# Two pairs of chunks at once through an FFN, with one PSUM bank left to the attention beside it

## The chip, the cores and the metric

The kernel runs on one core of a Trainium2 chip. The metric is the device time of one execution in microseconds (us), the median of several runs.

## The reference, cut to what matters

```python
# q, k, v: (4, 8, 768, 64) float32; w_in: 512 x 2048, w_out: 2048 x 512, handed over as float64
def _attn_ref(q, k, v):
    gamma = 1.0 - 2.0 ** (-5.0 - np.arange(H))
    for t in range(S):
        state = gamma[None, :, None, None] * state + np.einsum('bhd,bhe->bhde', k[:, :, t], v[:, :, t])
        y[:, :, t] = scale * np.einsum('bhd,bhde->bhe', q[:, :, t], state)
    ...
def _moe_ref(x, w_in, w_out):
    h = x @ w_in
    g = np.maximum(h, 0.0) + np.log1p(np.exp(-np.abs(h)))
    return (g @ w_out).astype(np.float32)
    ...
# x is y with its heads side by side: 3072 tokens x 512
```

A linear attention with a decay for each head is followed by a two-layer FFN with softplus between its layers.

## The kernel before

**Attention.** The 3072 tokens are 24 chunks of 128 (six for each of the four sequences). A chunk is worked in two halves of four heads; such a half is a *unit*, and there are 48, numbered in order. Within a unit, q times k gives scores, which are masked and multiplied by v; the state that came from earlier chunks is multiplied by q and added (`yp`); k times v is added up in PSUM (`stp`) as the next state. Units below `WHOLE` (12) do this in plain fp32 with transposes on TensorE. Later units split each operand into a high and a low part (fp32r) and sum the products; their q and k come as 32x32 blocks by small DMAs, 16 for a unit, and are transposed on VectorE. A unit's result is written into the ring `xring` as a high part `xh` and a low part `xl`.

**FFN.** `hidden(s)` multiplies a chunk of `w_in` (128 of the 2048 columns, `f`) with the tokens of one block in the ring, three products (high-high, high-low, low-high) for each of the four slices of 512, into a PSUM tile `hp`. `softplus(s)` makes `gh` and `gl` of it on VectorE, ScalarE and GpSimd. `second(s)`, run two steps later (`LAG`), multiplies these with `w_out` into accumulators of 128 tokens x 512. The blocks of tokens are 256, 256, six times 384, and 256 (`BLOCKS`). A step has two `f` for a block of 256 and one for 384, so 120 steps in all. Block 0 is interrupted: it goes through the first ten `f`, then block 1 runs through all 16 while the last weights arrive, then block 0 takes the rest and adds a stored partial sum. The weights come as float64 and are converted in pieces of one `f` (`convert_weights`), which takes all the engines but TensorE.

**PSUM.** Eight banks: two for `hp`, three accumulators `acc0` to `acc2`, two for the attention (`ps_a`, tag `a`, used in turn by transposes, scores and `yp`), one for the states.

**Order.** Attention runs in *ticks*: `PARTS` says at which tick of a unit each part of it comes (loads 24 ticks ahead or, from `THIRD` on, 40; operands at 0, scores at 8, new state at 12, outputs at 19 or 20), and a new unit begins every 16 ticks. The main loop walks over the FFN's steps and lets the ticks pass between them. For the first 32 steps (`ordered`), up to the end of block 2, a `plan` says how far the ticks are to get by each step, and a scheduler orders the instructions of every engine by a model of their times. From step 32 on the order of TensorE's instructions is fixed as written (`manual_schedule`), and `paced` deals out the ticks over the pieces of the steps, where a piece is one turn of `hidden` or of `second`, three matmuls. The other engines' orders come from the scheduler throughout.

Of the kernel before, what the change touches and what calls it, by code (L numbers as in the profile page):

```python
# [19 lines left out]
BLOCKS = (256, 256) + 6 * (384,) + (256,)  # L20
RING = 768
SPREAD = 9
# [5 lines left out]
TURN = 5  # L28
# [6 lines left out]
def decay_attention_then_softplus_ffn(ctx: ExitStack, tc: tile.TileContext, q, k, v, w_in, w_out, qtab, vtab, gtab, out):  # L35
# [7 lines left out]
    assert sum(BLOCKS) == B * S  # L43
    FIRST = np.cumsum((0,) + BLOCKS)
# [8 lines left out]
    ps_a = ctx.enter_context(tc.tile_pool(name="ps_a", bufs=2, space=bass.MemoryType.PSUM))  # L53
# [52 lines left out]

    xring = [attn.tile([P, ND, RING], F32R, name=nm) for nm in ("xh", "xl")]
    places, spans = {}, {}
    for i, size in enumerate(BLOCKS):
        at = (0, 256, 384, 0)[i] if i < 4 else 384 * (i % 2 == 0)  # L110
        order = {2: (1, 2, 0), 3: (2, 0, 1)}.get(i, range(size // C))
        spans[i] = slice(at, at + size), order
        for m, pos in enumerate(order):
            places[int(FIRST[i]) // C + m] = at + pos * C
# [17 lines left out]

    def block_tile(nm, n):
        home = {"pool": ffn, "tag": "part"} if n >= THIRD and (n - THIRD) % 3 == 0 else {"pool": attn, "tag": nm}
        if n < THIRD - 2:
            return home["pool"].tile([P, NJ, C // 32, 32], F32, name=f"{nm[0]}b", tag=home["tag"], bufs=2)
        at = nm, (n - THIRD) % 3
        if at not in rings:
            rings[at] = home["pool"].tile([P, NJ, C // 32, 32], F32, name=f"{nm[0]}b", tag=home["tag"], bufs=2)
        return rings[at]  # L140
# [27 lines left out]
    def load_ahead(n):  # L168
        if n >= THIRD:
            load_qk(n)  # L170
# [35 lines left out]

    def operands(n):
        b, c, hf = units[n]
        *rest, vn = loads.pop(n)
        if n < WHOLE:  # L210

            tp = ps_o.tile([P, 2, NJ, C], F32, name="tp", tag=f"acc{n % 2}") if n < 4 else ps_a.tile([P, 2, NJ, C], F32, name="tp", tag="a")
# [27 lines left out]
    def scores(n):  # L240
        kq = live[n][0]
        a = attn.tile([P, HH, C], F32, name="a")
        if n < WHOLE:
            sc = ps_a.tile([P, HH, C], F32, name="sc", tag="a")
            for h in range(HH):
                nc.tensor.matmul(sc[:, h, :], lhsT=kz[:, h % 2, h // 2, :], rhs=kq[:, h // 2, :], start=True, stop=True)
            nc.scalar.copy(a, sc)
        else:
            for j in range(NJ):
                sc = ps_a.tile([P, 2, 2, C], F32, name="sc", tag="a")  # L250
                for par in range(2):
                    nc.tensor.matmul(sc[:, par], lhsT=kq[:, 0, par, j, :], rhs=kq[:, 1:, par, j, :], start=True, stop=True)  # L252
                nc.vector.tensor_reduce(a[:, 2 * j:2 * j + 2, :], sc.rearrange("p h t c -> p h c t"), axis=mybir.AxisListType.X, op=ALU.add)  # L253
        nc.gpsimd.affine_select(a, a, pattern=[[0, HH], [1, C]], compare_op=ALU.is_ge, fill=0.0, base=0, channel_multiplier=-1)  # L254
        live[n].append(a)
        if n >= WHOLE:
            ah, al = (attn.tile([P, HH, C], F32R, name=nm) for nm in ("ah", "al"))
            nc.scalar.copy(ah, a)  # L258
            nc.gpsimd.tensor_tensor(al, a, ah.bitcast(F32), op=ALU.subtract)  # L259
            live[n][-1:] = [ah, al]  # L260
# [37 lines left out]
    def outputs(n):  # L298
        b, c, hf = units[n]
        kq, *rest, st = live.pop(n)  # L300
        off, g = places[n // 2], hf * NJ
        xh, xl = (x[:, g:g + NJ, off:off + C] for x in xring)
        if n < WHOLE:
            kn, vn, a = rest
            yp = ps_a.tile([P, NJ, C], F32, name="yp", tag="a")
# [10 lines left out]
        yp = ps_a.tile([D, 2, NJ, C], F32, name="yp", tag="a")  # L316
# [23 lines left out]
        ys = vn.rearrange("p h d -> p (h d)").rearrange("p (j c) -> p j c", j=NJ)  # L340
# [10 lines left out]

    def outputs_soon(n):
        if n >= WHOLE:
            stack_and_outputs(n)

    def outputs_late(n):
        if n < WHOLE:
            stack_and_outputs(n)

    PARTS = {-24: load_unit, -40: load_ahead, -8: decay, 0: operands, 8: scores, 12: new_state, 19: outputs_soon, 20: outputs_late}  # L360
# [11 lines left out]

    acc, part, hps, sps, gs = {}, {}, {}, {}, {}

    def hidden(s):
        i, fs = steps[s]
        xh, xl = (x[:, :, spans[i][0]] for x in xring)
        hp = hps[s] = ps_h.tile([P, len(fs), BLOCKS[i]], F32, name="hp", tag="hp")
        for k, d in ((k, d) for k in range(len(fs)) for d in range(ND)):
            wt = win[fs[k]].rearrange("p t (c f) -> p t c f", c=ND)  # L380
            nc.tensor.matmul(hp[:, k], lhsT=wt[:, 0, d, :], rhs=xh[:, d, :], start=d == 0, stop=False)  # L381
            nc.tensor.matmul(hp[:, k], lhsT=wt[:, 0, d, :], rhs=xl[:, d, :], start=False, stop=False)  # L382
            nc.tensor.matmul(hp[:, k], lhsT=wt[:, 1, d, :], rhs=xh[:, d, :], start=False, stop=d == ND - 1)  # L383
            yield
# [15 lines left out]

    def second(s):
        i, fs = steps[s]
        NT = BLOCKS[i] // P
        gh, gl = gs.pop(s)
        begins = s == 0 or steps[s - 1][0] != i
        ends = s + 1 == len(steps) or steps[s + 1][0] != i
        if begins:
            acc[i] = [ps_o.tile([P, DM], F32, name=f"acc{t}", tag=f"acc{t}") for t in range(NT)]
        for k, t in ((k, t) for k in range(len(fs)) for t in range(NT)):
            wt, ts = wout[fs[k]], slice(t * P, (t + 1) * P)  # L410
            nc.tensor.matmul(acc[i][t], lhsT=gh[:, k, ts], rhs=wt[:, 0], start=begins and k == 0, stop=False)  # L411
            nc.tensor.matmul(acc[i][t], lhsT=gh[:, k, ts], rhs=wt[:, 1], start=False, stop=False)  # L412
            nc.tensor.matmul(acc[i][t], lhsT=gl[:, k, ts], rhs=wt[:, 0], start=False, stop=ends and k == len(fs) - 1)  # L413
            if ends and (k, t) == (len(fs) - 1, NT - 1):
                write_out(i, fs)
            yield

    def write_out(i, fs):
        NT = BLOCKS[i] // P
        for t in range(NT):  # L420
            if fs[-1] < NF - 1:
                part[i, t] = ffn.tile([P, DM], F32, name="part")
                (nc.scalar.copy if t % 2 else nc.vector.tensor_copy)(part[i, t], acc[i][t])
                continue
            o = ffn.tile([P, DM], F32, name="o", tag="o")
            if (i, t) in part:
                nc.vector.tensor_tensor(o, acc[i][t], part.pop((i, t)), op=ALU.add)
            else:
                (nc.scalar.copy if t % 2 else nc.vector.tensor_copy)(o, acc[i][t])
            row = int(FIRST[i]) + list(spans[i][1]).index(t) * P  # L430
            nc.sync.dma_start(out[row:row + P, :], o)

    turns = [(0, 0, 2 * TURN), (1, 0, NF), (0, 2 * TURN, NF)]
    turns += [(i, 0, NF) for i in range(2, len(BLOCKS))]
    steps = []
    for i, a, b in turns:
        m = WIDE // BLOCKS[i]
        steps += [(i, tuple(range(f, f + m))) for f in range(a, b, m)]  # L440

    def ticks_for(i):

        return min(PERIOD * 2 * int(FIRST[i + 1] // C) + max(PARTS) - PERIOD + TICK + TICK * AHEAD, last_tick + TICK)

# [64 lines left out]
    starts = [s for s, (i, fs) in enumerate(steps) if fs[0] == 0]  # L510
    ordered = starts[3]
    plan = [0] * ordered
    for i in 1, 2, 3:
        a, b = starts[i - 1], starts[i]
        a, n = {1: (a + 1, b - a - 2), 2: (b - SPREAD, SPREAD), 3: (a + 1, b - a - 2)}[i]
        have, more = ticks_for(i - 1), ticks_for(i) - ticks_for(i - 1)
        for s in range(a, b):
            plan[s] = have + more // TICK * min(s - a + 1, n) // n * TICK

    def pieces_of(s):
        return len(steps[s][1]) * ND + len(steps[s - LAG][1]) * (BLOCKS[steps[s - LAG][0]] // P)

    paced = {}
    for a, b in zip(starts[3:], starts[4:]):
        i = steps[b][0]
        slots = [(s, t) for s in range(a + 1, b - 1) for t in range(pieces_of(s))]
        have, more = ticks_for(i - 1), ticks_for(i) - ticks_for(i - 1)
# [35 lines left out]
    for s, (i, fs) in enumerate(steps[:ordered]):  # L565
# [39 lines left out]
```

## Time and profile before

| | |
|---|---|
| median of 3 runs | 680.1 us (678.86 to 681.18) |
| the profiled execution | 680.08 us, span 678.4 us |
| granted TensorE clock, mean | 0.997 |
| TensorE busy (PE) | 659.6 us, 97% |
| VectorE, ScalarE, GpSimd busy | 413.0, 369.3, 313.9 us |
| DMA | 46.76 MB, most of it in the first 140 us |

The span is the profiled time from the first to the last instruction; the execution's own time is 1.7 us more. PE counts matmuls and PEld the loading of their stationary operands, which runs beside them. Matmuls are pipelined: a recorded one lasts longer than the distance to the next one, so the price of one in a stream is the distance from start to start. "<-" behind an idle time names what ended it. The ends of the slices on the page are 17 us apart.

### The profile page before, as it was taken

How to read it: one execution, taken by the hardware profiler on the slowest of the kernel's cores; microseconds unless marked ns; L12 is line 12 of the kernel's file. 1: busy time of each engine (PE TensorE's matmuls, PEld its weight loads, DVE VectorE, ACT ScalarE, POOL GpSimd, SP SyncE). 2: the span in 40 equal slices, each digit the busy share in tenths (PEclk: the TensorE clock that was granted, in tenths of full speed). 3: DMA queues.
4: the chain of work that ended last, by engine and by line, in shares of the span. 5: the costliest groups of instructions: out<-in, count | busy, mean ns of one | idle time of the engine just before them, and what ended most of it. 6: DMA issues, size and time to landing. Idle time of an engine off the chain costs nothing.

```text
span 678.4 us, 12865 instructions
## 1 busy us (share of the span) xinstructions
PE 659.6 (97%) x4146; PEld 600.6 (89%) x4146; DVE 413.0 (61%) x807; ACT 369.3 (54%) x844; POOL 313.9 (46%) x354
## 2 busy tenths in 40 slices
PE   7999899999999999999999999999999999999997
PEld 6888789997988898999999999999999899999996
DVE  5778698567566766674757655775666645432321
ACT  5878775545645555663656545654555635423221
POOL 5787666534534543534453525454435443232221
PEclk9999999999999999999999999999999999999999
DMA  9898652123221232221322222131322101000100
GB/s 241 222 287 238 186 141 65 26 70 76 53 39 37 46 88 38 42 45 36 78 47 38 49 66 45 31 57 34 79 38 52 23 8 56 1 1 1 46 1 32
DMA packets 153827, 46.76 MB, mean 69 GB/s; under 512 B 140448, under 2 KB 148640, under 8 KB 153760
## 3 DMA queue, kind: packets, MB, share of 16 engines
q1 hardware_dynamic: 153312, 45.93, 28.4%
q8 instruction: 33, 0.54, 0.3%
q14 instruction: 34, 0.28, 0.1%
q10 hardware_dynamic: 448, 0.01, 0.0%
HBM read 39.60 MB, written 6.29 MB: 68 GB/s over the span
## 4 chain that ended last, share of the span: by engine, by line
PE 62%; DMA 10%; DVE 8%; ACT 7%; SPq 5%; issue 4%; POOL 2%; ACTq 0%; DVEq 0%; POOLq 0%
PE hp L381 9%; PE acc L412 9%; PE acc L413 9%; PE acc L411 9%; PE hp L382 9%; PE hp L383 9%; SPq L150 4%; PE yp L322 4%; DMA win<-in_moe_w_in_dram 3%; DMA qb<-in_q_dram 2%; DMA kb<-in_k_dram 2%; PE sc L252 2%; DMA vn<-in_v_dram 1%; PE stp L274 1%; DMA qn<-in_q_dram 1%
## 5 line engine op out<-in xcount | busy, mean ns | idle before, releaser
L398 POOL TENSOR_TENSOR gl<-sp,gh 128x384 fp32r<-128x384 f32 (+1 forms) x120 | 129.9, 1083 | 213.0 <-ACT gh L396 182.7
L381 PE MATMUL hp<-xh,winhl 128*128 128x384 f32 (+1 forms) x576 | 186.9, 325 | 2.1 <-DVE sp L394 1.6
L383 PE MATMUL hp<-xh,winhl 128*128 128x384 f32 (+1 forms) x576 | 184.1, 320 | 0.0
L382 PE MATMUL hp<-xl,winhl 128*128 128x384 f32 (+1 forms) x576 | 183.4, 318 | 0.0
L411 PE MATMUL acc<-wouthl,gh 128*128 128x512 f32 x384 | 151.6, 395 | 0.0
L412 PE MATMUL acc<-wouthl,gh 128*128 128x512 f32 x384 | 151.2, 394 | 0.0
L413 PE MATMUL acc<-wouthl,gl 128*128 128x512 f32 x384 | 150.8, 395 | 0.2 <-POOL gl L398 0.2
L390 ACT ACTIVATE sp<-sp 128x384 f32<-128x384 f32 (+1 forms) x120 | 65.5, 546 | 135.7 <-DVE sp L389 133.4
L381 PEld LDWEIGHTS hp<-xh,winhl 128*128 128x128 f32 x576 | 108.8, 189 | 6.0 <-DVE sp L394 1.4
L382 PEld LDWEIGHTS hp<-xl,winhl 128*128 128x128 f32 x576 | 109.0, 189 | 3.4
L389 DVE TENSOR_SCALAR sp<-hp 128x384 uint32<-128x384 uint32 (+1 forms) x120 | 68.9, 575 | 67.8 <-PE hp L383 66.5
L383 PEld LDWEIGHTS hp<-xh,winhl 128*128 128x128 f32 x576 | 108.7, 189 | 0.2
L396 ACT CAST gh<-sp 128x384 fp32r<-128x384 f32 (+1 forms) x120 | 64.2, 535 | 75.1 <-DVE sp L394 54.2
L394 DVE SCALAR_TENSOR_TENSOR sp<-hp,sp 128x384 f32<-128x384 f32 (+1 forms) x120 | 69.2, 577 | 38.3 <-ACT sp L390 37.7
L413 PEld LDWEIGHTS acc<-wouthl,gl 128*128 128x128 f32 x384 | 71.8, 188 | 15.6 <-POOL gl L398 0.4
L412 PEld LDWEIGHTS acc<-wouthl,gh 128*128 128x128 f32 x384 | 72.2, 188 | 10.9
L411 PEld LDWEIGHTS acc<-wouthl,gh 128*128 128x128 f32 x384 | 72.2, 188 | 10.8
L254 POOL TENSOR_SCALAR_AFFINE_SELECT a<-a 128x512 f32<-128x512 f32 x48 | 35.7, 744 | 55.8 <-DVE a L253 49.6
L259 POOL TENSOR_TENSOR al<-a,ah 128x512 fp32r<-128x512 f32 x36 | 47.3, 1313 | 7.5 <-ACT ah L258 7.5
L224 DVE STREAM_TRANSPOSE kb<-kb 128x256 f32<-128x256 f32 x36 | 16.0, 445 | 56.6 <-DMA kb<-in_k_dram 46.0
L253 DVE TENSOR_REDUCE a<-sc 128x256 f32<-128x512 f32 x72 | 47.1, 681 | 5.2 <-PE sc L252 4.6
L258 ACT CAST ah<-a 128x512 fp32r<-128x512 f32 x36 | 22.3, 619 | 42.9 <-POOL a L254 42.9
(80 smaller groups left out, 912.1 us busy)
## 6 DMA issues: line engine op xcount, KB each, us to landing
win<-in_moe_w_in_dram SPq DMA_DIRECT2D x16, 512.0 KB, 4.6
wout<-in_moe_w_out_dram SPq DMA_DIRECT2D x16, 512.0 KB, 4.4
vn<-in_v_dram SPq DMA_DIRECT2D x48, 128.0 KB, 2.3
out_dram<-o SPq DMA_DIRECT2D x24, 256.0 KB, 2.1
kb<-in_k_dram SPq DMA_DIRECT2D x288, 16.0 KB, 1.7
qb<-in_q_dram SPq DMA_DIRECT2D x288, 16.0 KB, 1.7
vn<-in_k_dram SPq DMA_DIRECT2D x30, 128.0 KB, 2.3
qn<-in_q_dram SPq DMA_DIRECT2D x12, 128.0 KB, 4.2
```

The costliest lines, as they stand in the source:

```text
L259: nc.gpsimd.tensor_tensor(al, a, ah.bitcast(F32), op=ALU.subtract)
L381: nc.tensor.matmul(hp[:, k], lhsT=wt[:, 0, d, :], rhs=xh[:, d, :], start=d == 0, stop=False)
L382: nc.tensor.matmul(hp[:, k], lhsT=wt[:, 0, d, :], rhs=xl[:, d, :], start=False, stop=False)
L383: nc.tensor.matmul(hp[:, k], lhsT=wt[:, 1, d, :], rhs=xh[:, d, :], start=False, stop=d == ND - 1)
L389: nc.vector.tensor_scalar(sp.bitcast(U32), hps[s].bitcast(U32), 0x80000000, None, op0=ALU.bitwise_or)
L390: nc.scalar.activation(sp, sp, AF.Softplus)
L394: nc.vector.scalar_tensor_tensor(g, hps.pop(s), 0.0, g, op0=ALU.max, op1=ALU.add)
L396: nc.scalar.copy(gh, g)
L398: nc.gpsimd.tensor_tensor(gl, sps.pop(s), gh.bitcast(F32), op=ALU.subtract)
L411: nc.tensor.matmul(acc[i][t], lhsT=gh[:, k, ts], rhs=wt[:, 0], start=begins and k == 0, stop=False)
L412: nc.tensor.matmul(acc[i][t], lhsT=gh[:, k, ts], rhs=wt[:, 1], start=False, stop=False)
L413: nc.tensor.matmul(acc[i][t], lhsT=gl[:, k, ts], rhs=wt[:, 0], start=False, stop=ends and k == len(fs) - 1)
```

## The change

The tokens go in *pairs* of chunks, 256 tokens, of which there are 12. A turn of the FFN has two pairs in flight, so that a hidden matmul has 512 columns, and the two are half of the weights apart: in a turn over the first eight `f` (or the last eight) one pair ends and the next one begins. Pair 0 alone takes the first eight, pair 1 alone all 16, then pairs 0 and 2 the last eight, 2 and 3 the first eight, 3 and 4 the last, and so on, up to pair 11, which ends alone. There are 96 steps. Each pair in flight has two accumulators, so four banks hold accumulators, and one is left to the attention from unit 12 on. For the units before that the fourth accumulator's bank is the attention's second. The scores come in two parts, at ticks 7 and 10, and the outputs all come at tick 20. TensorE's order is fixed from step 12 on (the third turn). The results before splitting (`ys`) get a buffer of their own from unit 19 on, in place of `vn`; each tile of the result is written out as soon as its last matmul is in.

```diff
-BLOCKS = (256, 256) + 6 * (384,) + (256,)
-RING = 768
+TWO = 2 * C
+PLACES = 3
-TURN = 5
+TURN = 4
...
-    ps_a = ctx.enter_context(tc.tile_pool(name="ps_a", bufs=2, space=bass.MemoryType.PSUM))
+    ps_a = ctx.enter_context(tc.tile_pool(name="ps_a", bufs=1, space=bass.MemoryType.PSUM))
...
+    xring = [attn.tile([P, ND, PLACES * TWO], F32R, name=nm) for nm in ("xh", "xl")]
+    def place_of(p):
+        return p if p < PLACES else (1, 0, 2)[p % PLACES]
...
     def load_ahead(n):
-        if n >= THIRD:
+        if n > THIRD:
             load_qk(n)
...
+    def attention_bank(n, shape, name):
+        taken.append(n)
+        if n < WHOLE and len(taken) % 2:
+            return ps_o.tile(shape, F32, name=name, tag="acc3")
+        return ps_a.tile(shape, F32, name=name, tag="a")
...
+    def scores_of_pair(n, j):
+        kq = live[n][0]
+        if j == 0:
+            summed[n] = attn.tile([P, HH, C], F32, name="a")
+        sc = attention_bank(n, [P, 2, 2, C], "sc")
+        for par in range(2):
+            nc.tensor.matmul(sc[:, par], lhsT=kq[:, 0, par, j, :], rhs=kq[:, 1:, par, j, :], start=True, stop=True)
+        nc.vector.tensor_reduce(summed[n][:, 2 * j:2 * j + 2, :], sc.rearrange("p h t c -> p h c t"), axis=mybir.AxisListType.X, op=ALU.add)
...
-        yp = ps_a.tile([D, 2, NJ, C], F32, name="yp", tag="a")
+        yp = attention_bank(n, [D, 2, NJ, C], "yp")
...
-        ys = vn.rearrange("p h d -> p (h d)").rearrange("p (j c) -> p j c", j=NJ)
+        if n < THIRD:
+            ys = vn.rearrange("p h d -> p (h d)").rearrange("p (j c) -> p j c", j=NJ)
+        else:
+            ys = rings[("kn", "qn")[n % 2]].rearrange("p j i d -> p j (i d)")
...
-    PARTS = {-24: load_unit, -40: load_ahead, -8: decay, 0: operands, 8: scores, 12: new_state, 19: outputs_soon, 20: outputs_late}
+    PARTS = {-24: load_unit, -40: load_ahead, -8: decay, 0: operands, 7: scores_first, 8: scores_whole, 10: scores_second, 12: new_state, 20: stack_and_outputs}
...
+    turns = [((0,), 0, 2 * TURN), ((1,), 0, NF), ((0, 2), 2 * TURN, NF)]
+    turns += [((p, p + 1), *((0, 2 * TURN), (2 * TURN, NF))[p % 2]) for p in range(2, PAIRS - 1)]
+    turns += [((PAIRS - 1,), 2 * TURN, NF)]
+    for pairs, a, b in turns:
+        starts.append(len(steps))
+        m = WIDE // (len(pairs) * TWO)
+        steps += [(pairs, tuple(range(f, f + m))) for f in range(a, b, m)]
...
     def hidden(s):
-        i, fs = steps[s]
-        xh, xl = (x[:, :, spans[i][0]] for x in xring)
+        pairs, fs = steps[s]
+        at = sorted(place_of(p) for p in pairs)
+        at = slice(at[0], at[-1] + 1, max(1, at[-1] - at[0]))
+        xh, xl = (x.rearrange("p d (r t) -> p d r t", t=TWO)[:, :, at] for x in xring)
...
     def second(s):
+        for p in pairs:
+            if begins(s, p):
+                odd = p % 2 or p == 0
+                acc[p] = [ps_o.tile([P, DM], F32, name=f"acc{t}", tag=f"acc{t}") for t in ((0, 1) if odd else (2, 3))]
...
+            if last:
+                write_out(p, t, s < TURN)
...
-    ordered = starts[3]
+    ordered = starts[2]
...
-    for a, b in zip(starts[3:], starts[4:]):
-        i = steps[b][0]
-        slots = [(s, t) for s in range(a + 1, b - 1) for t in range(pieces_of(s))]
-        have, more = ticks_for(i - 1), ticks_for(i) - ticks_for(i - 1)
+    for p in range(3, PAIRS):
+        slots = [(s, t) for s in range(starts[p - 1], starts[p]) for t in range(pieces_of(s))]
+        have, more = ticks_for(p - 1), ticks_for(p) - ticks_for(p - 1)
         for t, slot in enumerate(slots):
             paced[slot] = have + more * (t + 1) // len(slots)
```

More of the change, by code (lines that the diff above doesn't have):

```diff
@@ L133, in block_tile @@
     def block_tile(nm, n):
-        home = {"pool": ffn, "tag": "part"} if n >= THIRD and (n - THIRD) % 3 == 0 else {"pool": attn, "tag": nm}
         if n < THIRD - 2:
-            return home["pool"].tile([P, NJ, C // 32, 32], F32, name=f"{nm[0]}b", tag=home["tag"], bufs=2)
+            return attn.tile([P, NJ, C // 32, 32], F32, name=f"{nm[0]}b", tag=nm, bufs=2)
         at = nm, (n - THIRD) % 3
         if at not in rings:
-            rings[at] = home["pool"].tile([P, NJ, C // 32, 32], F32, name=f"{nm[0]}b", tag=home["tag"], bufs=2)
+            if n == THIRD:
+                both = ffn.tile([P, 2, NJ, C // 32, 32], F32, name=f"{nm[0]}bys", tag="part")
+                rings[at], rings[nm] = both[:, 0], both[:, 1]
+            else:
+                rings[at] = attn.tile([P, NJ, C // 32, 32], F32, name=f"{nm[0]}b", tag=nm, bufs=2)
         return rings[at]
@@ L210, in operands @@
         if n < WHOLE:
-            tp = ps_o.tile([P, 2, NJ, C], F32, name="tp", tag=f"acc{n % 2}") if n < 4 else ps_a.tile([P, 2, NJ, C], F32, name="tp", tag="a")
+            tp = ps_o.tile([P, 2, NJ, C], F32, name="tp", tag=f"acc{n % 2}") if n < 4 else attention_bank(n, [P, 2, NJ, C], "tp")
             for t, x in enumerate(rest):
@@ L238, in operands, with mask, scores_whole @@
         live[n] = [kq, vhl, tokens_of(n)[1], vn]
-    def scores(n):
+    def mask(a):
+        nc.gpsimd.affine_select(a, a, pattern=[[0, HH], [1, C]], compare_op=ALU.is_ge, fill=0.0, base=0, channel_multiplier=-1)
+    def scores_whole(n):
+        if n >= WHOLE:
+            return
         kq = live[n][0]
         a = attn.tile([P, HH, C], F32, name="a")
-        if n < WHOLE:
[L244 to L260, printed above, removed]
@@ new lines, in scores_whole @@
+        sc = attention_bank(n, [P, HH, C], "sc")
+        for h in range(HH):
+            nc.tensor.matmul(sc[:, h, :], lhsT=kz[:, h % 2, h // 2, :], rhs=kq[:, h // 2, :], start=True, stop=True)
+        nc.scalar.copy(a, sc)
+        mask(a)
+        live[n].append(a)
+    summed = {}
+    def scores_of_pair(n, j):
[6 more added lines that the diff above has]
+        nc.vector.tensor_reduce(summed[n][:, 2 * j:2 * j + 2, :], sc.rearrange("p h t c -> p h c t"), axis=mybir.AxisListType.X, op=ALU.add)
@@ L262, in decay_attention_then_softplus_ffn, with scores_first, scores_second @@
+    def scores_first(n):
+        if n >= WHOLE:
+            scores_of_pair(n, 0)
+    def scores_second(n):
+        if n < WHOLE:
+            return
+        scores_of_pair(n, 1)
+        a = summed.pop(n)
+        mask(a)
+        ah, al = (attn.tile([P, HH, C], F32R, name=nm) for nm in ("ah", "al"))
+        nc.scalar.copy(ah, a)
+        nc.gpsimd.tensor_tensor(al, a, ah.bitcast(F32), op=ALU.subtract)
+        live[n] += [ah, al]
     began = {}
@@ L401, in second @@
     def second(s):
-        i, fs = steps[s]
-        NT = BLOCKS[i] // P
+        pairs, fs = steps[s]
         gh, gl = gs.pop(s)
[L405 to L415, printed above, removed]
-            yield
@@ L418, in write_out @@
[L418 to L431, printed above, removed]
@@ L435, in decay_attention_then_softplus_ffn @@
[L435 to L444, printed above, removed]
+        places = sorted(place_of(p) for p in pairs)
+        for p in pairs:
+            if begins(s, p):
+                odd = p % 2 or p == 0
+                acc[p] = [ps_o.tile([P, DM], F32, name=f"acc{t}", tag=f"acc{t}") for t in ((0, 1) if odd else (2, 3))]
@@ new lines, in second @@
+        for k, p, t in ((k, p, t) for k in range(len(fs)) for p in pairs for t in range(2)):
+            at = places.index(place_of(p)) * TWO + t * P
+            first, last = begins(s, p) and k == 0, ends(s, p) and k == len(fs) - 1
+            wt, ts, to = wout[fs[k]], slice(at, at + P), acc[p][t]
+            nc.tensor.matmul(to, lhsT=gh[:, k, ts], rhs=wt[:, 0], start=first, stop=False)
+            nc.tensor.matmul(to, lhsT=gh[:, k, ts], rhs=wt[:, 1], start=False, stop=False)
+            nc.tensor.matmul(to, lhsT=gl[:, k, ts], rhs=wt[:, 0], start=False, stop=last)
+            if last:
+                write_out(p, t, s < TURN)
+            yield
@@ new lines, in write_out @@
+    def write_out(p, t, partial):
+        to = acc[p][t]
+        if partial:
+            part[t] = ffn.tile([P, DM], F32, name="part")
+            (nc.scalar.copy if t % 2 else nc.vector.tensor_copy)(part[t], to)
+            return
+        o = ffn.tile([P, DM], F32, name="o", tag="o")
+        if p == 0:
+            nc.vector.tensor_tensor(o, to, part.pop(t), op=ALU.add)
+        else:
+            (nc.scalar.copy if t % 2 else nc.vector.tensor_copy)(o, to)
+        row = p * TWO + t * P
+        nc.sync.dma_start(out[row:row + P, :], o)
@@ L563, in paced_stages @@
                 slot += 1
-    for s, (i, fs) in enumerate(steps[:ordered]):
+    for s, (pairs, fs) in enumerate(steps[:ordered]):
         if s == TURN:
```

52 lines of the change are left out of this document (22 added, 30 removed).

## The prediction

> **What bounds the kernel now.** I read the page first (span, busy time, the slices), then busy time by stretch, then single matmuls in the timeline, then the waits around the one PSUM tile that the change takes a bank from.
>
> ```profile
> span 678.4 us, 12865 instructions
> ...
> PE 659.6 (97%) x4146; PEld 600.6 (89%) x4146; DVE 413.0 (61%) x807; ACT 369.3 (54%) x844; POOL 313.9 (46%) x354
> ...
> PE   7999899999999999999999999999999999999997
> ```
>
> TensorE is the bound: 97% of the span, and nines nearly throughout. The other engines are at 46 to 61%. So only two things count: how long the stream of matmuls is, and how long TensorE stands still in it. The time by stretch (columns: PE, PEld, DVE, ACT, POOL busy, each with its instructions; granted clock; DMA share; GB/s):
>
> ```profile
> 0.00:20.00 20.00, 15.91 (x82) 13.74 (x83) 10.71 (x31) 11.30 (x23) 11.43 (x25) 0.91 0.95 254
> 20.00:100.00 80.00, 74.86 (x540) 68.78 (x540) 63.90 (x113) 63.89 (x135) 57.97 (x70) 1.00 0.76 209
> 100.00:120.00 20.00, 20.00 (x133) 18.34 (x132) 17.25 (x30) 11.73 (x21) 14.46 (x13) 1.00 0.34 79
> 120.00:300.00 180.00, 175.24 (x1108) 158.85 (x1107) 118.55 (x234) 100.73 (x245) 82.68 (x91) 1.00 0.25 51
> 300.00:565.00 265.00, 264.03 (x1635) 241.67 (x1635) 165.38 (x338) 147.59 (x357) 116.51 (x129) 1.00 0.22 47
> 565.00:678.40 113.40, 109.59 (x658) 99.27 (x656) 37.26 (x64) 34.02 (x67) 30.88 (x29) 1.00 0.04 14
> ```
>
> Idle TensorE is the stretch less its PE column: 4.1 us in the first 20, 5.1 us to 100, none to 120, 4.8 us from 120 to 300, 1.0 us to 565, and 3.8 us at the end, which is the last write-out. The granted clock is 1.00 after the first 20 us, so no part of this is a slow clock. The kernel could be freed of some 10 us of idle at most; the rest has to come out of the stream.
>
> **The stream.** The start of a matmul to the start of the next one is its price (the recorded durations overlap):
>
> ```profile
> 401.09 0.40 PE L411 MATMUL acc<-wouthl,gh 128*128 128x512 f32 x1
> ...
> 401.79 0.34 PE L381 MATMUL hp<-xh,winhl 128*128 128x384 f32 x1
> ...
> 402.86 0.33 PE L381 MATMUL hp<-xh,winhl 128*128 128x384 f32 x1
> 647.95 0.28 PE L381 MATMUL hp<-xh,winhl 128*128 128x256 f32 x1
> ...
> 649.03 0.28 PE L381 MATMUL hp<-xh,winhl 128*128 128x256 f32 x1
> L381 PE MATMUL hp<-xh,winhl 128*128 128x384 f32 x384 | 131.9, 344 | 0.0
> L381 PE MATMUL hp<-xh,winhl 128*128 128x256 f32 x192 | 55.0, 287 | 2.1 <-DVE sp L394 1.6 <-ACT xh L313 0.5
> ```
>
> Three of 512 columns lie between 401.09 and 401.79, so 0.233 us each; six of 384 between 401.79 and 402.86, 0.178 each; nine of 256 between 647.95 and 649.03, 0.120 each. The price is about 0.44 ns for a column and 8 to 9 ns for being a matmul. The number of columns does not change: every token meets every weight as before. The number of matmuls does. Before there are 3 x 384 = 1152 of 384 columns and 3 x 192 = 576 of 256 (the two rows, and as many in lines 382 and 383), 1152 x 0.178 + 576 x 0.120 = 274.2 us. After, single pairs run for 8, 16 and 8 of the weight columns' chunks, 32 x 12 = 384 matmuls of 256, and ten two-pair turns of 8 chunks, 10 x 8 x 12 = 960 of 512: 960 x 0.233 + 384 x 0.120 = 269.8 us. That is **4.4 us less**. The second product keeps its 1152 matmuls of 512. That two pairs can lie apart in the ring (places 0 and 2) makes the moving operand a two-level one; the score matmul at line 252 reads such an operand already, and I put it at nothing.
>
> The Trainium skill, page "TensorE: Matmul & The Clock Gate", section "Wait — 56ns, not 53.3ns?", gives a warm matmul N/2.4 GHz and a fixed 2.5 ns or so. By that estimate the 384 matmuls saved would be worth about 1 us. The rows above show more than three times that fixed part here, and the sum goes by them.
>
> **Softplus and gl.** 96 steps instead of 120, each over 512 elements; less work for DVE, ACT and POOL, none of it on the path, as idle TensorE of 1.0 us in the 265 us from 300 on shows. Nothing. The same holds for write-out: an accumulator comes up again only one turn later with hidden matmuls between.
>
> **Fixed order from step 12 instead of step 32.** Step 12 will start near 118 us, where before the scheduler's order went on to about 232 us. The stretch from 120 to 300 lost 4.8 us, and a stall also costs the pipeline's refill, 0.395 - 0.233 = 0.16 us (the 512-column matmul's record against its price; 395 is the mean of one at line 411). With some eight stalls that is 6 us. From 300 to 565 the order was fixed and lost 1 us. If the new order is as smooth, **6 us go**.
>
> **One bank for attention.** This is the cost. In the fixed part every unit now takes its scores of pair j=0, of pair j=1 and its yp from one bank in turn; before there were two. So the next unit's first scores wait until ACT has copied yp out (line 342), and the second scores until DVE has reduced the first (line 253). In a turn of two pairs there are 8 steps of 8 pieces (4 hidden, 4 second) and 64 ticks, one tick behind each piece. yp stands at tick 20, the next unit's first scores at 16 + 7 = 23: three pieces later. Both lie in the second half of the same step, so three pieces are nine matmuls of 512, 9 x 0.233 = 2.10 us. How long does the copy take? Before, a unit at the same place, behind the first second piece of its step:
>
> ```profile
> 320.19 0.40 PE L322 MATMUL yp<-al,vhl 128*64 128x128 f32 x4
> 320.43 0.45 PE L411 MATMUL acc<-wouthl,gh 128*128 128x512 f32 x1
> ...
> 319.39 0.52 ACT L390 ACTIVATE sp<-sp 128x384 f32<-128x384 f32 x1 [2.47 <-DVE sp L389]
> 319.97 0.41 ACT L231 CAST kq<-qb 64x256 fp32r<-64x256 f32 x1
> 320.40 0.40 ACT L232 CAST kq<-qb 64x256 fp32r<-64x256 f32 x1
> 320.82 0.40 ACT L231 CAST kq<-qb 64x256 fp32r<-64x256 f32 x1
> 321.25 0.53 ACT L294 CAST st<-stp 64x128 fp32r<-64x128 f32 x2
> 321.81 0.41 ACT L232 CAST kq<-qb 64x256 fp32r<-64x256 f32 x1
> 322.24 0.74 ACT L342 COPY vn<-yp 64x256 f32<-64x256 f32 x2
> ...
> 323.46 0.63 PE L252 MATMUL sc<-kq 128*128 128x256 f32 x4
> 323.89 0.69 DVE L253 TENSOR_REDUCE a<-sc 128x256 f32<-128x512 f32 x1
> ```
>
> The last yp matmul leaves at 320.43, but ACT first casts the q blocks of the unit after the next (lines 231 and 232, free as soon as yp's state products have read them) and the new state (line 294), 2.2 us in all, and the two copies end at 322.98. That is 2.55 us behind yp. Nothing waited, since the scores at 323.46 went into the other bank. In the new place the scores would come at 320.43 + 2.10 = 322.53 and stand until about 323.05, some 0.5 us. The softplus ahead on ACT is longer with 512 elements, so I take 0.55 us. This queue forms where the unit has state products, stacks a new state, and has the q blocks loaded far ahead: units 18 to 45 are 28, less the 4 of a sequence's first chunk and the 4 of its last, 20 units. 20 x 0.55 = **11 us more**. The waits of before, in which only the second scores came behind yp, five ticks later, were short:
>
> ```profile
> who waited for it (us, times):
>   PEld sc L252: 1.6, 3
>   PE sc L252: 0.9, 1
> ```
>
> That is the whole wait of the scores for line 342, in three places. Lower bound of the new term: these 0.9 us. Upper bound: every one of 36 units at 0.55 and the odd write-out cast (0.58) in half of them, 30 us. I take 11, the counted case.
>
> The Trainium skill, page "PSUM — Partial Sum Buffer", section "Summary: rules for kernel authors", says that to read PSUM while a matmul runs one gives the matmul another bank. The rows above agree: copies and the next scores stand apart by bank before. By this rule the change is a cost in each unit.
>
> The reduce between the two scores: scores start 323.46, reduce ends 324.58, 1.12 us. The new distance is two scores (0.24) and 2.10, 2.34 us. It is covered unless DVE is 1.2 us behind; DVE is busy 62% from 300 to 565, so sometimes. 0 to 8 us, I take 2. From the second scores to yp there remain ten ticks, some 8 us, for
>
> ```profile
> L254 POOL TENSOR_SCALAR_AFFINE_SELECT a<-a 128x512 f32<-128x512 f32 x48 | 35.7, 744 | 55.8 <-DVE a L253 49.6
> L259 POOL TENSOR_TENSOR al<-a,ah 128x512 fp32r<-128x512 f32 x36 | 47.3, 1313 | 7.5 <-ACT ah L258 7.5
> L258 ACT CAST ah<-a 128x512 fp32r<-128x512 f32 x36 | 22.3, 619 | 42.9 <-POOL a L254 42.9
> ```
>
> and the reduce, 0.74 + 1.31 + 0.62 + 0.68 = 3.4 us: covered.
>
> **Units 12 to 17 in fixed order.** Their blocks are still loaded 24 ticks ahead, and late loads now stop TensorE instead of being stepped round:
>
> ```profile
> DVE kb L224 <- DMA kb<-in_k_dram: 46.0, 27, 3.6
> POOL vn L205 <- DMA vn<-in_v_dram: 25.4, 21, 5.9
> ```
>
> Waits of up to 3.6 and 5.9 us, today beside other work. On SP the 16 block loads of a unit stand one behind the other as before. Between nothing and 10 us for six units; I take 3, since most such waits have cover of a few ticks. The separate buffer for ys frees vn sooner, so the load of v no longer waits for line 344: worth nothing after 300 us. The moves by a tick (first scores 8 to 7, second to 10, outputs 19 to 20) pass no DMA of their own: these parts issue only matmuls and the ACT, DVE and POOL work costed above, and the loads that SP issues stay at their ticks, four behind the outputs instead of five.
>
> **The early part.** Turn 0 has 4 steps instead of 5, so the last weights are needed one step sooner, and a step of 256 columns is 24 x 0.120 + 12 x 0.233 = 5.7 us:
>
> ```profile
> L99 ACT CAST winhl<-w x16: 601/620/625, 13.3 to 116.2; 128x512 fp32r<-128x512 f32 x16
> L99 ACT CAST wouthl<-w x16: 601/620/631, 16.5 to 120.3; 128x512 fp32r<-128x512 f32 x16
> ```
>
> The last weights are cast at 116.2 and 120.3 us, just before use, with DVE at 17.25 of 20 us there. If the conversions can't come sooner TensorE stands up to 5.7 us; if they can, nothing (a gain is excluded, all of this work stays). I take 2.
>
> **The sum.** The profiled execution took 680.08 us (span 678.4 and 1.7 around it), which is the median of the runs, 680.1. 680.1 - 4.4 - 6 + 11 + 2 + 3 + 2 = **687.7 us**, slower by 1.1%.
>
> **The rivals.** (1) *The copy is in time.* If ACT's order comes out with the copies ahead of the casts, as they need only 0.74 us, the bank is free 1.3 us before the scores. The point is 2.10 us from yp's end to the copies' end. Then the 11 us vanish and most of the other waits with them: 680.1 - 4.4 - 6 + 1 = about 671 us, faster. For it: the waits of 0.9 us before. Against it: the casts stood ahead by readiness, which this change does not touch. Chance 0.30. (2) *Late operands stop TensorE.* Fixed order starts while loads and conversions still compete; the 3 + 2 + 2 us become 10 + 6 + 8: about 705 us. For it: the waits of up to 5.9 us. Against it: 1 us idle in 265 us of fixed order. Chance 0.10. (3) *Gain and wait cancel.* The wait is met in half of the units only: 680.1 - 10.4 + 6 + 5 = 681 us. Chance 0.13.
>
> **How the numbers follow.** The forecast has chance 0.47, own range 682 to 700. A change of under 0.3% (678 to 682 us) can't be told from none here. Slower 0.47 + 0.10 = 0.57; same 0.13; faster 0.30. The range that leaves out a tenth at each end reaches into both neighbours, 669 to 702 us.
>
> **What would show it.** 1344 hidden matmuls with 512-column ones 0.23 us apart; TensorE waits at line 252 for ACT's line 342, some 20 of about half a us, in the fixed part; little idle between 120 and 300 us beyond these; the last weights' casts near 114 to 118 us with TensorE waiting for them. I am wrong if line 342 runs ahead of lines 231 and 232, or ends within 2.1 us of yp: then the time falls to about 671.

## The result, and the profile after

The changed kernel took 702.7 us (700.0 to 704.9), the kernel before 679.8: 1.033 times as long, 95% interval 1.029 to 1.038. It was forecast slower, but by 1.1%; the time lies 15.0 us above the forecast of 687.7 and 0.7 us above the range of 669 to 702. The changed kernel's page, the lines that answer to those shown of before:

```profile
span 700.0 us, 11837 instructions
...
PE 662.1 (95%) x3762; PEld 556.8 (80%) x3762; DVE 417.4 (60%) x756; ACT 361.1 (52%) x799; POOL 310.1 (44%) x330
...
PE   7899998789899989999999989999999999999997
```

There are 384 fewer matmuls (3762 for 4146), but TensorE's busy time did not fall, because matmuls behind a wait or at a slow clock are busy longer (both are shown below). TensorE is idle 37.9 us where it was 18.8. Of the 19.1 us that came on top, most have one owner. What the changed kernel's copies of yp (line 374, line 342 before) held up:

```profile
who waited for it (us, times):
  PEld sc L273: 28.3, 26
  PE sc L273: 17.0, 25
```

The second line counts idle TensorE: 17.0 us in 25 waits, where before it was 0.9 us in one. By the prediction's estimate each wait costs 0.16 us more for the pipeline to fill again, so some 21 us in all. One of them in detail, ScalarE first, then TensorE:

```profile
354.51 0.63 ACT L432 ACTIVATE sp<-sp 128x512 f32<-128x512 f32 x1 [3.11 <-DVE sp L431]
355.05 0.39 ACT L241 CAST kq<-qb 64x256 fp32r<-64x256 f32 x1
355.46 0.41 ACT L242 CAST kq<-qb 64x256 fp32r<-64x256 f32 x1
355.89 0.40 ACT L241 CAST kq<-qb 64x256 fp32r<-64x256 f32 x1
356.32 0.53 ACT L323 CAST st<-stp 64x128 fp32r<-64x128 f32 x2
356.88 0.41 ACT L242 CAST kq<-qb 64x256 fp32r<-64x256 f32 x1
357.30 0.74 ACT L374 COPY kbys<-yp 64x256 f32<-64x256 f32 x2
```
```profile
355.40 0.45 PE L456 MATMUL acc<-wouthl,gh 128*128 128x512 f32 x1
...
357.31 0.40 PE L458 MATMUL acc<-wouthl,gl 128*128 128x512 f32 x1
358.10 0.50 PE L273 MATMUL sc<-kq 128*128 128x256 f32 x2 [0.40 <-ACT kbys L374]
```

The six casts stand ahead of the two copies, as they did in the kernel before; the copies end at 358.04, 2.64 us behind yp, and the scores, whose place in the stream came at 357.54, start at 358.10. This is the forecast's wait in its forecast place.

The second owner was not forecast. The fixed order begins with step 12, at 115.6 us. Behind its fifth piece stands yp of unit 12, and it waits 4.6 us, from 121.5 to 126.1; the matmuls behind it run at about half the pace (from start to start 0.42 to 0.43 us, then 0.23 again):

```profile
PE yp L351 <- ACT ah L287: 4.6, 1, 4.6
```
```profile
128.94 0.63 PE L458 MATMUL acc<-wouthl,gl 128*128 128x512 f32 x1
129.36 0.63 PE L456 MATMUL acc<-wouthl,gh 128*128 128x512 f32 x1
...
130.33 0.40 PE L456 MATMUL acc<-wouthl,gh 128*128 128x512 f32 x1
130.56 0.40 PE L457 MATMUL acc<-wouthl,gh 128*128 128x512 f32 x1
```

The Trainium skill, page "TensorE: Matmul & The Clock Gate", section "What's actually happening", has the array at 2.4 GHz or, after an idle window of some 3.4 us, at 1.2. By that estimate 512 columns take 427 ns when slow, and the rows' 0.42 to 0.43 us agree. The window alone does not describe this kernel: the slow pace also follows single waits of 2.5, 2.0 and 1.8 us (before 178.2, 142.3 and 415.5 us), though not the one of 1.9 us before 250.4. The shortest of them:

```profile
415.49 0.50 PE L273 MATMUL sc<-kq 128*128 128x256 f32 x2 [1.78 <-ACT kbys L374]
...
417.24 0.63 PE L425 MATMUL hp<-xh,winhl 128*128 128x512 f32 x1
417.67 0.63 PE L423 MATMUL hp<-xh,winhl 128*128 128x512 f32 x1
```

### The profile page after: what moved, and what is told of

It is laid out like the page before. It is cut to its first block, busy times and chain, and to the rows that moved or that the text cites. A ratio compares the mean times of both kernels' runs of the same rounds, so it can differ in the third digit from the quotient of the medians.

```text
span 700.0 us, 11837 instructions
## 1 busy us (share of the span) xinstructions
PE 662.1 (95%) x3762; PEld 556.8 (80%) x3762; DVE 417.4 (60%) x756; ACT 361.1 (52%) x799; POOL 310.1 (44%) x330
## 4 chain that ended last, share of the span: by engine, by line
PE 52%; ACT 12%; SPq 8%; DVE 8%; DMA 7%; issue 4%; ACTq 0%; POOL 0%; DVEq 0%; POOLq 0%
PE hp L423 9%; PE hp L425 9%; PE hp L424 9%; SPq L151 7%; PE acc L456 7%; PE acc L457 7%; PE acc L458 7%; ACT kq L242 3%; DVE sp L431 3%; ACT kq L241 3%; PE sc L273 3%; DMA kb<-in_k_dram 2%; DMA qb<-in_q_dram 2%; PE stp L303 2%; PE yp L351 2%
## 5 line engine op out<-in xcount | busy, mean ns | idle before, releaser
L440 POOL TENSOR_TENSOR gl<-sp,gh 128x512 fp32r<-128x512 f32 x96 | 124.0, 1292 | 265.4 <-ACT gh L438 263.1
L423 PE MATMUL hp<-xh,winhl 128*128 128x512 f32 (+1 forms) x448 | 163.0, 364 | 1.3 <-ACT winhl L97 0.8
L424 PE MATMUL hp<-xl,winhl 128*128 128x512 f32 (+1 forms) x448 | 162.9, 364 | 0.0
L425 PE MATMUL hp<-xh,winhl 128*128 128x512 f32 (+1 forms) x448 | 162.0, 362 | 0.2 <-POOL winhl L98 0.2
L432 ACT ACTIVATE sp<-sp 128x512 f32<-128x512 f32 x96 | 60.4, 630 | 138.6 <-DVE sp L431 138.5
L431 DVE TENSOR_SCALAR sp<-hp 128x512 uint32<-128x512 uint32 x96 | 65.7, 685 | 105.1 <-PE hp L425 103.2
L425 PEld LDWEIGHTS hp<-xh,winhl 128*128 128x128 f32 x448 | 85.2, 190 | 14.1 <-POOL winhl L98 0.6
L423 PEld LDWEIGHTS hp<-xh,winhl 128*128 128x128 f32 x448 | 85.1, 190 | 12.6 <-ACT winhl L97 1.0
L438 ACT CAST gh<-sp 128x512 fp32r<-128x512 f32 x96 | 59.5, 619 | 57.7 <-PE acc L457 30.0
L436 DVE SCALAR_TENSOR_TENSOR sp<-hp,sp 128x512 f32<-128x512 f32 x96 | 64.9, 677 | 26.4 <-ACT sp L432 25.6
L273 PEld LDWEIGHTS sc<-kq 128*128 128x128 f32 x144 | 25.2, 191 | 34.6 <-ACT kbys L374 11.4
L273 PE MATMUL sc<-kq 128*128 128x256 f32 x144 | 32.3, 307 | 18.5 <-ACT kbys L374 7.0
```

Source lines behind the costliest of these rows:

```text
L423: nc.tensor.matmul(to, lhsT=wt[:, 0, d, :], rhs=xh[:, d], start=d == 0, stop=False)
L424: nc.tensor.matmul(to, lhsT=wt[:, 0, d, :], rhs=xl[:, d], start=False, stop=False)
L425: nc.tensor.matmul(to, lhsT=wt[:, 1, d, :], rhs=xh[:, d], start=False, stop=d == ND - 1)
L431: nc.vector.tensor_scalar(sp.bitcast(U32), hps[s].bitcast(U32), 0x80000000, None, op0=ALU.bitwise_or)
L432: nc.scalar.activation(sp, sp, AF.Softplus)
L436: nc.vector.scalar_tensor_tensor(g, hps.pop(s), 0.0, g, op0=ALU.max, op1=ALU.add)
```

## The experiments

Three questions: is the time lost to the single bank and the copies (theory A), to the start of the fixed order (B, later D), or does a cure only move the wait (C)? Two stretches tell the first two apart. Busy time in 118 to 180 and 180 to 620 us (PE first, granted clock third from the end), for the kernel before:

```profile
118.00:180.00 62.00, 60.35 (x395) 54.82 (x394) 40.77 (x78) 33.37 (x77) 29.09 (x31) 1.00 0.26 56
180.00:620.00 440.00, 435.92 (x2690) 398.01 (x2689) 267.52 (x539) 236.71 (x571) 190.23 (x210) 1.00 0.20 42
```

and for the changed one:

```profile
118.00:180.00 62.00, 51.42 (x267) 41.91 (x266) 37.78 (x68) 30.05 (x71) 24.63 (x25) 0.90 0.21 42
180.00:620.00 440.00, 425.25 (x2362) 350.86 (x2361) 268.54 (x491) 225.53 (x522) 185.66 (x188) 0.99 0.21 43
```

Idle TensorE went from 1.7 to 10.6 us in the first and from 4.1 to 14.8 us in the second.

Each ratio is to runs of the kernel before on the same chip in the same session; their median lay between 679.8 and 681.3 us, so differences between medians of two sessions are good to a us or two.

| kernel | median us | ratio to before (95%) |
|---|---|---|
| changed | 702.7 | 1.033 (1.029 to 1.038) |
| copies first | 679.1 | 0.997 (0.994 to 1.001) |
| scores a tick later | 676.5 | 0.995 (0.993 to 0.996) |
| two attention banks | 672.6 | 0.989 (0.987 to 0.991) |
| fixed from the fourth turn | 710.3 | 1.044 (1.041 to 1.046) |
| late start alone | 690.9 | 1.014 (1.011 to 1.017) |
| scores later + late start | **667.5** | 0.981 (0.979 to 0.984) |
| the same, conversions earlier | 667.6 | 0.980 (0.978 to 0.982) |
| copies first + scores later | 682.8 | 1.003 (1.001 to 1.005) |
| scores later, half width | 684.6 | 1.006 (1.004 to 1.008) |
| before, one bank | 761.5 | 1.120 (1.117 to 1.123) |
| before, fixed from block 2 | 682.7 | 1.003 (1.001 to 1.004) |

**Copies first.**

```diff
+    def behind(inst, n):   # inst goes after unit n's copies in the engine's order
+        if n in copied:
+            tc.add_manual_dep(inst.ins, copied[n].name, ...NoSync...)
-            nc.scalar.copy(kq[own, 1, par], qt[own])
+            behind(nc.scalar.copy(kq[own, 1, par], qt[own]), n - 2)
...
-            nc.scalar.copy(st[own, par], s)
+            behind(nc.scalar.copy(st[own, par], s), n)
```

> The changed kernel with one thing more: on ScalarE the casts of the q blocks of unit n+2 and of unit n's new state may not stand ahead of unit n's two copies of yp. Theory A (the single bank is held by the copies, which stand behind 2.2 us of casts in ScalarE's queue): the scores' waits for the copies, 21.2 us in all in the changed kernel's trace, fall to about 2 us, since the copies then end some 1.0 us behind yp where the scores come 2.1 us behind it; 702.7 - 19 = about 684 us. Theory B (the loss is at the start of the fixed order, and the copies' waits only take up slack that would be lost anyway): within 3 us of 702.7. Theory C (the casts, moved back, become what the next unit waits for): the waits move to the first scores or to yp, and the time stays above 695 us.

It came to 679.1, 24 us less where 19 were expected. ScalarE's order alone is worth this; no part of the attention was moved to another tick. Idle TensorE behind the copies (line 380 here) fell from 17.0 to 1.1 us, in one place:

```profile
  PE sc L279: 1.1, 1
```

Some of theory C is there too: the scores (line 279 here) now wait for VectorE's reduce,

```profile
PE sc L279 <- DVE a L280: 4.0, 3, 3.2
```

4.0 us in three places.

**Scores a tick later.**

```diff
-    PARTS = {..., 7: scores_first, 8: scores_whole, 10: scores_second, ...}
+    PARTS = {..., 8: scores_both, 11: scores_second, ...}   # both: scores_whole and scores_first
```

> The changed kernel with the first scores at tick 8 instead of 7 and the second at 11 instead of 10, so one piece (0.69 us) more between yp and the next scores. Theory A: the waits of 0.56 us fall to nothing, the longer ones by 0.69 us each; of 21.2 us some 6 stay, so about 688 us. Theory B: no change beyond 3 us. Theory C: what is taken from the distance between second scores and yp (ten ticks to nine) comes back as waits of yp for al.

676.5, a gain of 26 us, more than the 15 expected: the longer waits went as well, where only 0.69 us of each had been counted on. The copies' line in this kernel (378):

```profile
who waited for it (us, times):
  PEld sc L273: 0.7, 1
  PE sc L273: 0.3, 1
```

So the tick did more than add distance. The orders of the other engines came out anew with it, and VectorE's waits for the blocks of k, which stood behind some of the long waits (the section on the prediction shows one), are shorter. The changed kernel first, then with the tick:

```profile
DVE kbys L234 <- DMA kbys<-in_k_dram: 18.1, 8, 4.2
```
```profile
DVE kbys L234 <- DMA kbys<-in_k_dram: 7.0, 7, 1.7
```

How much of the 26 us belongs to the distance and how much to the new order was not separated.

**Two attention banks.**

```diff
-    ps_a = ctx.enter_context(tc.tile_pool(name="ps_a", bufs=1, ...
+    ps_a = ctx.enter_context(tc.tile_pool(name="ps_a", bufs=2, ...
-                acc[p] = [... for t in ((0, 1) if odd else (2, 3))]
+                acc[p] = [... for t in ((0, 1) if odd else (2,))]
...   # and so in second and write_out
```

> The changed kernel with two banks for the attention again, at the same ticks. The eighth bank comes from leaving something out: of each even pair but pair 0 both tiles of 128 tokens are added into one accumulator, so their result is their sum; the matmuls, casts and write-outs are as many as before. Theory A: no score waits for a copy, and 702.7 - 21 = about 682 us. Theory B: within 3 us of 702.7. What is then left over the kernel before is the start of the fixed order, less the 4 us of the wider matmuls.

672.6: 30 us less than with one bank at the same ticks. This kernel leaves out the separate sums of an even pair's two tiles, as said. In the later stretch TensorE's busy time is

```profile
180.00:620.00 440.00, 435.03 (x2435) 364.74 (x2433) 267.12 (x494) 230.57 (x531) 187.47 (x187) 1.00 0.21 44
```

5.0 us idle, not nothing: with two banks in turn it is the second scores that come behind yp, and in seven places they still wait, 6.0 us in all. The first stretch gains too (58.35 us busy, 3.7 idle), so the bank had a part in the trouble at the start. The changed kernel's trace shows which: there unit 12's second scores, at 121.0 us, could not start before the reduce of the first, which VectorE ran only from 120.25 to 120.94, and ah, for which yp then waits, is made from these second scores.

**Where the fixed order begins.** First the other way:

```diff
-    ordered = starts[2]
+    ordered = starts[3]
...   # and the ranges of the plan and of paced, one turn later
```

> The changed kernel with TensorE's order fixed from the fourth turn (step 20) instead of the third (step 12). In the changed kernel TensorE loses some 16 us between 118 and 180 us, 4.8 of it in one wait of yp for ah, 2.1 for gh, and some 3 at a lower clock behind these. Theory B: this comes from fixing the order there, and with the scheduler's order 8 to 11 us of it go: about 693 us. Theory A: the single bank's waits are independent of it and stay at 15 us and more after 180 us. If neither the order nor the bank at this place matters: 702.

710.3: theory B as put there is wrong. The loss moved along with the start and grew:

```profile
118.00:160.00 42.00, 38.27 (x191) 31.80 (x191) 24.22 (x43) 19.46 (x43) 17.41 (x17) 0.96 0.20 44
160.00:205.00 45.00, 36.49 (x186) 29.73 (x186) 22.59 (x45) 19.08 (x46) 16.07 (x17) 0.85 0.20 36
```

3.7 us idle in the first of these stretches and 8.5 in the second, at a clock of 0.85. The copies' waits stay, 17.0 us in all, as theory A had it. So it is not the early place that hurts but the joint, where the scheduler's order of TensorE ends and the written one begins. A reading that fits, but was not tested by itself: the scheduler's model puts the engines elsewhere than the chip does, and the written order takes no account of how late they are. In the changed kernel yp of unit 12 is among the attention's first parts behind the joint. So the ticks were held back instead:

```diff
     def ticks_for(p):
-        return min(PERIOD * 4 * (p + 1) + max(PARTS) - PERIOD + TICK + TICK * AHEAD, last_tick + TICK)
+        return min(PERIOD * 4 * (p + 1) + max(PARTS) - PERIOD + TICK + TICK * (AHEAD if p != 2 else 0), last_tick + TICK)
```

> The scores a tick later, and eight ticks less done when the fixed order begins at step 12 (the attention's lead over the third turn is taken away, so the third turn deals out 72 ticks and unit 12's yp comes six to seven pieces into it instead of behind the fourth). Theory D (the 4.8 us in which yp of unit 12 waits for ah, and the eight slow matmuls behind it, come from yp standing right at the start of the fixed order, while VectorE and GpSimd still finish the last weights): most of these 4.8 + 1.6 us go, 676.5 - 5 = about 671 us. Theory E (unit 12's chain is late by more than that, or the hidden matmuls now wait for unit 11's result): within 2 us of 676.5.

> The changed kernel with the lead of eight ticks taken away at step 12 and the scores left at ticks 7 and 10. Theory D: the 4.8 us wait of unit 12's yp and the slow matmuls behind it go, 5 to 8 us less than 702.7, about 696 us; the waits of the first scores for the copies stay near 20 us. If the two causes were one (the copies late only because the start threw the engines out of step): the copies' waits go too, and it comes near 676 us.

With the scores later 667.5, 9 us less; alone 690.9, 11.8 less. The two edits act on two causes, and nearly add up: 26.2 + 11.8 = 38.0 by themselves, 35.2 together. With the late start alone TensorE still waits 16.2 us for the copies. The stretches say the same. Scores later alone, late start alone, and both:

```profile
118.00:180.00 62.00, 53.70 (x289) 44.04 (x288) 38.32 (x71) 32.00 (x75) 25.55 (x26) 0.94 0.22 45
180.00:620.00 440.00, 438.42 (x2468) 367.71 (x2467) 258.07 (x499) 232.88 (x533) 187.24 (x191) 1.00 0.21 44
```
```profile
118.00:180.00 62.00, 59.02 (x332) 47.84 (x331) 41.77 (x78) 34.05 (x80) 29.09 (x30) 1.00 0.27 54
180.00:620.00 440.00, 423.85 (x2356) 349.76 (x2355) 264.91 (x485) 224.45 (x519) 180.95 (x183) 1.00 0.20 42
```
```profile
118.00:180.00 62.00, 60.60 (x342) 49.83 (x341) 42.81 (x80) 35.58 (x84) 29.65 (x30) 1.00 0.26 52
180.00:620.00 440.00, 438.63 (x2454) 367.72 (x2453) 254.31 (x491) 230.16 (x524) 185.20 (x188) 1.00 0.21 44
```

The first cure leaves 8.3 us of idle time in the first stretch and 1.6 in the second; the other leaves 3.0 and 16.2; both leave 1.4 and 1.4. The granted clock in the first stretch, 0.90 in the changed kernel, is 1.00 with the late start.

**Fixed order alone, on the kernel before.**

```diff
-    ordered = starts[3]
+    ordered = starts[2]
...   # and the ranges of the plan and of paced, one block earlier
```

> The kernel before with TensorE's order fixed from block 2 (step 16, near 143 us) instead of block 3 (step 32, near 232 us); blocks, banks and ticks as before. The prediction put 6 us of gain on fixing the order earlier. Theory F (a fixed order with two banks is smooth wherever it starts): 3 to 6 us faster, about 675 us. Theory D (where it starts, the attention's chain is late and TensorE stands still, at a lower clock behind it): the gain is used up, 680 us or slower, with a wait of several us within the first unit's steps.

682.7, slower by a quarter of a percent. The joint again: a hidden matmul waits for unit 13's xl, and the stretch behind is slow:

```profile
PE hp L382 <- DVE xl L344: 2.8, 1, 2.8
```
```profile
143.00:160.00 17.00, 13.31 (x63) 11.01 (x62) 9.99 (x17) 6.00 (x14) 8.10 (x8) 0.80 0.30 70
```

Here a late load has a part in it: xl, made at 152.93 us, stands on VectorE behind a transpose that waited for its blocks.

```profile
151.06 0.45 DVE L224 STREAM_TRANSPOSE kb<-kb 128x256 f32<-128x256 f32 x1 [2.10 <-DMA qb<-in_q_dram]
```

**One bank alone, on the kernel before.**

```diff
-    ps_a = ctx.enter_context(tc.tile_pool(name="ps_a", bufs=2, ...
+    ps_a = ctx.enter_context(tc.tile_pool(name="ps_a", bufs=1, ...
```

> The kernel before with one attention bank instead of two and nothing else changed (the eighth bank lies idle). Its two scores of a unit stand one right behind the other, so the second must wait for the reduce of the first: 1.12 us from the first scores' start, less their 0.24, at least 0.9 us for each of the 24 units in its fixed part and about as much for the 12 before. Theory A (what the bank costs is the distance on TensorE between neighbours in it, against the time of the reader): 680 + 30 = about 710 us, more where VectorE is behind. If a single bank were no matter by itself: within 3 us of 680.

761.5, 81 us more where 30 were expected. The waits for the reduce are 36.3 us of idle TensorE in 28 places, 1.3 us each where 0.9 in 36 places was counted:

```profile
PE sc L252 <- DVE a L253: 36.3, 28, 2.4
```

The rest was not counted: units 0 to 11 need the bank for transposes, scores and yp, and the mean granted clock is 0.969. How much of the 81 us falls to each was not separated. That one bank cost 81 us here and 30 in the changed kernel goes with the new ticks of the scores, but the early units' second bank and the pairs differ as well.

**Both cures of the copies.** The two edits above together.

> Both cures at once: copies of yp ahead of the casts on ScalarE, and the scores a tick later (8 and 11). The tick alone left 0.4 us of first scores' waits, 4.3 of second scores' waits for the reduce and 4.8 at the first yp of the fixed order. Theory A: the waits for the copies were the whole difference, and either cure is enough: the same as with the tick alone, 676.5 us within 2 us. Theory C (the casts, moved back, come to stand before the next scores or in VectorE's way): 2 to 4 us more than with the tick alone, since the copies-first kernel had 5.5 us of waits for the reduce.

682.8, 6 us worse than the tick alone. Theory C, and more of it than expected: the casts now run behind the copies, and the VectorE operations that follow on them (lines 335, 249, 253 and 386 here) come right in front of the reduce of the first scores.

```profile
PEld sc L279 <- DVE a L280: 18.5, 28, 2.8
PE sc L279 <- DVE a L280: 7.6, 4, 2.4
```

In 28 places the loading of the scores' stationary operand waits for the reduce, in four of them TensorE stands idle. A cure that is right alone can be wrong beside another.

**Half width.**

```diff
-            nc.tensor.matmul(to, lhsT=wt[:, 0, d, :], rhs=xh[:, d], ...)
+            for r in range(len(pairs)):
+                nc.tensor.matmul(to[:, r], lhsT=wt[:, 0, d, :], rhs=xh[:, d, r], ...)
...   # and so for the other two products
```

> The scores a tick later, and each hidden matmul of 512 columns cut into two of 256 with the same stationary operand, 960 matmuls more. By the rows of the kernel before (0.120 us for 256 columns, 0.233 for 512) that is 960 x 0.007 to 0.0085 = 7 to 8 us more than 676.5: about 684 us. If a matmul's fixed part were the 2.5 ns that the Trainium skill gives (page TensorE: Matmul & The Clock Gate, section Wait — 56ns, not 53.3ns?), 2.4 us more: about 679 us.

684.6, 8.2 us more than with the full width: 8.5 ns for each of 960 matmuls. The rows' price holds, and the Trainium skill's figure of 2.5 ns does not fit this stream. The traces' own distances make the price higher still: 0.120 us from start to start for 256 columns and 0.227 for 512 (medians over all of each kind) make 13 ns for each further matmul, 12.5 us. Other losses were smaller with half width: TensorE is idle 20.6 us instead of 22.2, at a mean granted clock of 0.998 instead of 0.992.

**Conversions earlier.**

```diff
-EARLY = 2
+EARLY = 4
```

> The best version so far (scores a tick later, late start) with the weights converted four chunks ahead instead of two. In its trace some 2.4 us of TensorE's idle time between 100 and 118 us waits for the last weights (lines 97 and 98). If the conversions' place in the program sets when they run: 1 to 2 us less than 667.5. If VectorE's load does (it is busy nine tenths there): no change, or up to 2 us more, since conversions then stand ahead of the attention.

667.6, no change. The casts of the last weights moved by 0.3 us:

```profile
L97 ACT CAST wouthl<-w x16: 602/616/647, 16.8 to 117.3; 128x512 fp32r<-128x512 f32 x16
```
```profile
L97 ACT CAST wouthl<-w x16: 601/618/647, 16.7 to 117.0; 128x512 fp32r<-128x512 f32 x16
```

(First without, then with the edit.) Their place in the program is not what sets their time; that it is VectorE's load was not shown.

## Why the prediction was right or wrong

The sign, the place and the mechanism of the main term were right: the scores wait for the copies, the copies stand behind the casts, and a tick or ScalarE's order takes the wait away. Two terms of the sum failed, the size of the one bank's cost and the gain from the earlier fixed order. Step by step:

*The stream*, 4.4 us of gain: the half-width kernel puts 384 matmuls at 384 x 8.5 ns = 3.3 us, the medians of the distances (0.120, 0.174 and 0.227 us) put it at 5.6. Right within what the rows can carry. The price of "8 to 9 ns for being a matmul" is less sure than it looks, since the few rows shown give 7 to 8.5 and the medians 13.

*One bank*, 11 us: mis-sized, the first of the two steps that failed; measured, it is the 21 us above. The price of the common wait was right: 0.55 us forecast, and in 16 of the 25 waits about 0.40 us idle and 0.16 to fill again. The count was not: 25 waits instead of 20. Units 14 to 16, and 22, 23, 34 and 35 of a sequence's last chunk, waited as well, while 44 and 45 did not. Nor was the mean wait the common one: the other nine waits, of 0.5 to 2.5 us, are 10.7 of the 17.0 us. The long ones come from elsewhere. Here is one of 1.8 us of idle in the changed kernel, VectorE and then ScalarE:

```profile
410.79 0.45 DVE L234 STREAM_TRANSPOSE kbys<-kbys 128x256 f32<-128x256 f32 x1 [4.12 <-DMA kbys<-in_k_dram]
411.16 0.65 DVE L431 TENSOR_SCALAR sp<-hp 128x512 uint32<-128x512 uint32 x1
```
```profile
411.90 0.63 ACT L432 ACTIVATE sp<-sp 128x512 f32<-128x512 f32 x1 [4.50 <-DVE sp L431]
...
414.69 0.74 ACT L374 COPY kbys<-yp 64x256 f32<-64x256 f32 x2
```

A transpose for a later unit, whose result is first read 37 us later, waits 4.1 us for its DMA; the softplus behind it on VectorE is late, ScalarE's casts after that, and the copies last. The kernel before had such waits too, up to 3.6 us, and so has the one with two banks again, up to 3.7, with 5.0 us of idle TensorE in all from 180 to 620 us; so a second bank hides most of them. The prediction took the least case for the mean, though it had named the upper end of 30.

*Fixed order*, 6 us of gain, and *units 12 to 17*, 3 us of loss: the second step that failed. I read the smoothness of 300 to 565 us as a property of the fixed order, and it is one only behind the joint. Measured in the stretch 118 to 180: 10.6 us idle for 1.7. Of these 10.6 us, 4.9 are yp of unit 12 right behind the joint, which no term of the sum had; 2.0 are a wait for gh before 142.3, 0.8 one for the reduce, and 2.9 two waits for the copies, which are among the 25 above. The late loads that I named are there too: the longer of these two, 2.5 us before 178.2, stands behind a transpose on VectorE that waited for its blocks,

```profile
173.47 0.45 DVE L234 STREAM_TRANSPOSE kb<-kb 128x256 f32<-128x256 f32 x1 [3.26 <-DMA kb<-in_k_dram]
```

so these 3 us were about the right size. And the stalls were long enough to cost clock, for which the sum had no term: "no part of this is a slow clock" was read from the kernel before and did not carry over. With the late start and the scores later, half of the gain is there: 1.4 us idle from 118 to 180 and 1.4 from there to 620, against 1.7 and 4.1 before, which is 3.0 us less.

*The reduce*, 2 us, was about right as a wait: the second scores waited 1.4 us for it. What the sum did not see is its part in unit 12's wait at the joint. *The early part*, 2 us of loss, was too much: the changed kernel's page gives 0.8 and 0.2 us of idle for the last weights,

```profile
L423 PE MATMUL hp<-xh,winhl 128*128 128x512 f32 (+1 forms) x448 | 163.0, 364 | 1.3 <-ACT winhl L97 0.8
...
L425 PE MATMUL hp<-xh,winhl 128*128 128x512 f32 (+1 forms) x448 | 162.0, 362 | 0.2 <-POOL winhl L98 0.2
```

and all idle time up to 118 us is 8.7 us, where before it was 9.2. Rival 2 came nearest in its time, 705 us, by luck: it kept 11 us for the copies' waits, where some 21 were lost, and made up for it with 24 us of late operands, most of which the trace does not show. Rival 1, the copies in time, is what the new order on ScalarE and the single tick make of this kernel, 679.1 and 676.5 us where the rival said 671. Both still have the loss at the joint, which the rival did not foresee; with the tick and the late start together the time is 667.5.

## What to carry to other kernels

When a buffer is taken away, measure two distances: on the engine that reuses it, from the last use to the next, and on the engine that frees it, from the last use to the freeing instruction's end with all that its queue puts ahead. Here 2.1 us stood against 2.6, and one more piece between them turned a kernel 3.3% slower into one half a percent faster. Take the second distance from several units, not from the best one: nine late units of 25 cost more than the other 16. Where a written order takes over from a scheduled one, leave slack right behind the joint, and price a stall that reaches a few microseconds with the slow matmuls that follow.

## What the runs showed of the hardware that was not expected

Stalls of a few microseconds cost clock as well as time. Behind the wait of 4.6 us a handful of matmuls of 512 columns stood 0.43 us apart, and so they did behind a single wait of 1.8 us; over the 62 us with 10.6 us idle the granted clock was 0.90. The kernel before with one bank, where TensorE never waited longer than 3.0 us at once, ran its whole span at 0.969, against 0.997. Idle time alone undercounts such a kernel: its span is 82 us longer, and 57 of them are idle.
